# Decode attention over 537 MB of K and V: the first tile in halves with K in two pieces, and three halvings on VectorE in the last three tiles

## The chip, the cores and the metric

One core of one Trainium2 chip. The metric is device time in microseconds (us) of a whole execution; a run states the median of its timed executions. Each changed kernel was timed in alternating rounds with the kernel before on the same chip.

## The reference

```
B, H, Sq, Skv, Dh = 8, 32, 1, 4096, 128          # q, k, v in bf16
scores = einsum('bhqd,bhkd->bhqk', q, k) * Dh**-0.5
attn   = softmax(scores)
out    = einsum('bhqk,bhkd->bhqd', attn, v)
```

One query per head against 4096 keys: every byte of K and V is read once, 536.9 MB in all, and hardly any arithmetic is done per byte.

## The kernel before

A tile is eight heads: K and V are 8.39 MB each (128 partitions x 256 rows x 128), and there are 32 tiles. VectorE multiplies K by q and halves the products by additions; TensorE sums the rest with an identity matrix into PSUM; VectorE reduces that to scores; ScalarE makes the weights; TensorE multiplies V by them. K and V share a pool of three buffers.

```
SLOTS = 3                                          # K and V tiles in flight, in one pool
cuts = {
    ("k", 0): [C // 4, C // 4, C // 2],            # C = 256 rows of a partition
    ("k", NT - 2): [C // 2] * 2,
    ("k", NT - 1): [C // 4, C // 4, C // 2],
    ("v", NT - 1): [C // 2, C // 4, C // 8, C // 16, LAST // 2, LAST // 4, LAST // 4],
}
def load(kind, t):                                 # on the SP queue
    ...
        dma = nc.sync.dma_start(buf[:, c0 : c0 + n, :], src[t, :, c0 : c0 + n, :])
        ...
        if kind == "k" and t == 0 and c0 == n:     # q goes out behind the first piece of K
            nc.sync.dma_start(q_all[:], q_n)

def width_of(t, lo):                               # halve on VectorE down to this width
    return D // 8 if lo == C // 2 and 0 < t < NT - 3 else D // 2

def product(t, lo, hi):                            # VectorE: K*q, then the halvings
    ...
def sum_over_d(t, lo, hi):                         # TensorE: width/ds matmuls, ds = 512/(hi-lo)
    ...

for t in range(NT):
    loop = 0 < t <= LT                             # LT = NT - 3
    if not loop:                                   # tile 0 and the last two
        if t + 1 < NT: load("k", t + 1)
        load("v", t)
    first = HALF if loop else Q
    product(t, 0, first)
    ...
    if loop:                                       # halves
        sum_over_d(t, 0, HALF); product(t, HALF, C); sum_over_d(t, HALF, C)
        scores_of(t, 0, HALF)
        values_loop(t - 1)
        load("k", t + 1)
        load("v", t)                               # needs the buffer of K of tile t
        scores_of(t, HALF, C)
    else:                                          # quarters
        ...
    weights_of(t)
```

## Time and profile before

| | before |
|---|---|
| device time, median (range of 6) | 1250.97 us (1250.81 to 1251.15) |
| span of the profiled execution | 1249.5 us (its device time: 1251.34) |
| HBM traffic | 536.94 MB read, 430 GB/s over the span |
| busy: VectorE, TensorE, ScalarE | 81%, 61%, 13% |
| DMA | nine tenths or more in all slices but the last |

How to read it: 430 GB/s averaged over the whole span is nearly the 433.5 GB/s of the steady stretch. The lines for this are in the prediction.

### The profile page before, as it was taken

The page shows a single profiled execution, that of the slowest core. Times are in us where ns is not written, and L with a number is a line of the kernel's source. Part 1 is how long each engine was busy: PE and PEld are TensorE (multiplying, and loading weights), DVE is VectorE, ACT ScalarE, POOL GpSimd, SP SyncE. Part 2 cuts the span into 40 slices and gives each one's busy share as a digit, 9 for nine tenths or more (in the row PEclk, how much of TensorE's full clock was granted, in tenths as well). Part 3 has the DMA queues.
Part 4 walks back from the last instruction along what each step waited for, and adds up shares of the span by engine and source line. Part 5 has one row for each costly group of instructions (what it writes and reads, how often), then busy time and mean ns, then how long its engine had stood idle before and what let it go on. Part 6 is the DMA issues. An engine that isn't in the chain of part 4 may idle for free. (4 is left out here: it accounts for less than half of the span.)

```text
span 1249.5 us, 10534 instructions
## 1 busy us (share of the span) xinstructions
PE 761.4 (61%) x3004; PEld 284.3 (23%) x3004; DVE 1010.6 (81%) x379; ACT 166.1 (13%) x433; POOL 4.5 (0%) x24
## 2 busy tenths in 40 slices
PE   3356457554586555766557665577655676556855
PEld 1122122221222212222122222122221222212312
DVE  7877987778977789777797777987779877798694
ACT  0111011111011110111101111011110111101111
POOL 1000000000000000000000000000000000000000
PEclk9786798777887777878678777887867877778867
DMA  9999999999999999999999999999999999999998
GB/s 405 436 436 435 436 429 424 426 436 437 436 432 435 435 434 434 435 435 426 431 436 435 426 430 436 435 434 437 433 432 430 433 437 432 433 432 425 429 442 339
DMA packets 11430, 537.30 MB, mean 430 GB/s; under 512 B 1808, under 2 KB 2064, under 8 KB 2320
## 3 DMA queue, kind: packets, MB, share of 16 engines
q1 hardware_dynamic: 11072, 536.94, 99.5%
q8 instruction: 14, 0.23, 0.1%
q10 hardware_dynamic: 336, 0.07, 0.0%
q14 instruction: 8, 0.07, 0.0%
HBM read 536.94 MB, written 0.07 MB: 430 GB/s over the span
## 5 line engine op out<-in xcount | busy, mean ns | idle before, releaser
L189 DVE TENSOR_TENSOR kt<-kt,qb 128x16384 bf16<-128x16384 bf16 (+1 forms) x70 | 556.8, 7955 | 156.8 <-DMA kt<-in_k_dram 150.1
L207 PE MATMUL ps<-kt,ident 128*128 128x512 bf16 x688 | 253.2, 537 | 416.3 <-DVE kt L195 415.9
L290 PE MATMUL av<-vt,w 128*32 x1740 | 425.3, 397 | 4.4
L195 DVE TENSOR_TENSOR kt<-kt 128x4096 bf16<-128x4096 bf16 (+1 forms) x126 | 382.7, 3037 | 4.3
L290 PEld LDWEIGHTS av<-vt,w 128*32 x1740 | 173.3, 100 | 262.1 <-issue 118.9
L207 PEld LDWEIGHTS <-ident 128*128 128x128 bf16 x688 | 80.0, 125 | 583.0 <-DVE kt L195 444.7
L244 ACT ACTIVATE e<-sc,nmax 128x256 bf16<-128x256 f32 x32 | 16.2, 508 | 708.0 <-DVE nmax L238 708.0
L251 ACT ACTIVATE w<-e,mine 128x256 bf16<-128x256 bf16 x256 | 105.6, 495 | 1.1
L219 DVE TENSOR_REDUCE sc<-ps 128x128 f32<-128x512 f32 (+1 forms) x70 | 48.1, 687 | 57.0 <-PE ps L207 57.0
L347 ACT ACTIVATE comb<-av 32x512 bf16<-32x512 f32 (+1 forms) x32 | 18.8, 586 | 327.3 <-PEq L280 320.9
L276 PE MATMUL av<-vt,w 128*32 128x512 bf16 x116 | 47.1, 498 | 14.5 <-issue 13.3
L367 PE MATMUL op<-comb,pick 32*16 32x128 bf16 (+1 forms) x128 | 12.2, 213 | 21.9 <-ACT comb L347 21.9
L276 PEld LDWEIGHTS av<-vt,w 128*32 128x32 bf16 x116 | 6.9, 101 | 54.7 <-issue 54.7
L175 PE MATMUL qp<-qg,heads 8*128 8x128 bf16 x32 | 7.0, 217 | 16.7 <-ACT qg L173 16.7
L367 PEld LDWEIGHTS <-pick 32*16 32x16 bf16 (+1 forms) x128 | 8.7, 83 | 28.9 <-issue 28.5
L231 DVE TENSOR_REDUCE pmax<-sc 128x1 f32<-128x256 f32 x32 | 13.4, 420 | 1.1
L318 PE MATMUL av<-vt,w 128*32 128x512 bf16 x188 | 13.7, 417 | 0.0
L173 ACT ACTIVATE qg<-qh 8x128 bf16<-8x128 f32 x32 | 8.5, 267 | 33.5 <-PE qh L169 33.5
L169 PE MATMUL qh<-q_all,ident 128*8 128x128 bf16 x32 | 7.2, 225 | 8.7 <-DMA q_all<-in_q_dram 8.3
L177 ACT ACTIVATE qb<-qp 128x128 bf16<-128x128 f32 x32 | 8.9, 278 | 9.7 <-PE qp L175 9.7
L339 DVE RECIPROCAL rz<-zp 16x1 f32<-16x1 f32 x16 | 2.3, 147 | 8.1 <-PE zp L332 8.1
L233 DVE TENSOR_SCALAR spread<-same,pmax 128x32 f32<-128x32 f32 x32 | 7.7, 242 | 1.1
(30 smaller groups left out, 45.7 us busy)
## 6 DMA issues: line engine op xcount, KB each, us to landing
kt<-in_k_dram SPq DMA_DIRECT2D x4, 4096.0 KB, 23.8
kt<-in_k_dram SPq DMA_DIRECT2D x4, 2048.0 KB, 12.3
vt<-in_v_dram SPq DMA_DIRECT2D x1, 4096.0 KB, 33.1
vt<-in_v_dram SPq DMA_DIRECT2D x1, 2048.0 KB, 37.6
vt<-in_v_dram SPq DMA_DIRECT2D x1, 1024.0 KB, 39.7
vt<-in_v_dram SPq DMA_DIRECT2D x1, 512.0 KB, 40.5
vt<-in_v_dram SPq DMA_DIRECT2D x31, 26.2
kt<-in_k_dram SPq DMA_DIRECT2D x29, 28.7
```

The source lines that it names most:

```text
L189: nc.vector.tensor_tensor(out=part, in0=part, in1=qb[:].to_broadcast([P, hi - lo, D]), op=ALU.mult)
L195: nc.vector.tensor_tensor(out=part[:, :, 0:n], in0=part[:, :, 0:n], in1=part[:, :, n : 2 * n], op=ALU.add)
L207: nc.tensor.matmul(ps[:], lhsT=ident[:], rhs=kt[:, lo:hi, s * ds : (s + 1) * ds], start=(s == 0), stop=(s == n - 1),)
L219: made = nc.vector.tensor_reduce(out=scs[t][:, lo:hi], in_=ps, axis=AX.X, op=ALU.add)
L231: nc.vector.tensor_reduce(out=pmax[:], in_=sc[:], axis=AX.X, op=ALU.max)
L244: nc.scalar.activation(out=e[:], in_=sc[:], func=ACT.Exp, bias=nmax[:, 0:1], scale=scale, accum_out=esums[t // R][:, t % R : t % R + 1],)
L251: nc.scalar.activation(out=w[:, :, g, :], in_=e_g, func=ACT.Copy, scale=mine[:, 0, g : g + 1])
L276: pe.matmul(av, lhsT=wf[:, i * nw : (i + 1) * nw], rhs=vf[:, i * nv : (i + 1) * nv], **how)
L290: pe.matmul(av, lhsT=wf[:, bass.ds(ow + i * nw, nw)], rhs=vf[:, bass.ds(ov + i * nv, nv)], start=False, stop=False,)
L318: nc.tensor.matmul(avs[t][j * AG : (j + 1) * AG, :], lhsT=w[:, i, :, :], rhs=vt[:, c0 : c0 + CB, :], start=(i < TG), stop=(j not in group[ ...
L347: nc.scalar.activation(out=comb[0:n, :, :], in_=av[0:n, :, :], func=ACT.Copy)
L367: nc.tensor.matmul(ops[n][:], lhsT=pick[0:e, m, r, :], rhs=comb[0:e, m, :], start=(r == 0 and m == 0), stop=(r == R - 1 and m == CB - 1 an ...
```

## The change

Its intent: tile 0 takes the form of the tiles in the loop (two halves, the second with three halvings), so that VectorE and TensorE do fewer small pieces there, and the last three tiles trade slow waits for TensorE (16 or 8 matmuls) for short additions on VectorE.

```
-        ("k", 0): [C // 4, C // 4, C // 2],
+        ("k", 0): [C // 2] * 2,
...
-        return D // 8 if lo == C // 2 and 0 < t < NT - 3 else D // 2
+        return D // 8 if lo == (C // 2 if t <= LT else 3 * C // 4) else D // 2
...
+            halves = t <= LT
             loop = 0 < t <= LT
...
-            first = HALF if loop else Q
+            first = HALF if halves else Q
...
-            if loop:
+            if halves:
                 sum_over_d(t, 0, HALF)
                 product(t, HALF, C)
                 sum_over_d(t, HALF, C)
                 scores_of(t, 0, HALF)
...
-                values_loop(t - 1)
-                load("k", t + 1)
-                load("v", t)
+                if loop:
+                    values_loop(t - 1)
+                    load("k", t + 1)
+                    load("v", t)
                 scores_of(t, HALF, C)
```

q still goes out behind the first piece of K, which is now 4 MB instead of 2 MB.

More of the change, by code (lines that the diff above doesn't have):

```diff
@@ L129 @@
     nc.gpsimd.memset(w_last[:], 0.0)
+    LT = NT - 3
     loads = {}
@@ L299, in values_loop @@
         loops.append(loop)
-    LT = NT - 3
     def values_of(t, lo, hi):
@@ L404 @@
                 load("v", t)
-            first = HALF if loop else Q
+            first = HALF if halves else Q
             product(t, 0, first)
-            if not loop:
+            if not halves:
                 sum_over_d(t, 0, first)
@@ L440 @@
                 values_of(t - 1, 0, C)
-            if not loop:
+            if not halves:
                 scores_of(t, HALF + Q, C)
```

## The prediction

> **What bounds the kernel now.** I read the page's top first: which engine is full.
>
> ```profile
> PE 761.4 (61%) x3004; PEld 284.3 (23%) x3004; DVE 1010.6 (81%) x379; ACT 166.1 (13%) x433; POOL 4.5 (0%) x24
> DMA  9999999999999999999999999999999999999998
> HBM read 536.94 MB, written 0.07 MB: 430 GB/s over the span
> ```
>
> No compute engine is full, and the DMA engines are busy in every slice. VectorE's 81% is near enough that I checked whether it ever holds the transfers up. The idle time ahead of each tile's first product says no: in the steady state VectorE waits for K.
>
> ```profile
> 81.31 8.69 DVE L189 TENSOR_TENSOR kt<-kt,qb 128x16384 bf16<-128x16384 bf16 x1 [5.14 <-DMA kt<-in_k_dram]
> 121.38 8.69 DVE L189 TENSOR_TENSOR kt<-kt,qb 128x16384 bf16<-128x16384 bf16 x1 [6.61 <-DMA kt<-in_k_dram]
> 160.12 8.69 DVE L189 TENSOR_TENSOR kt<-kt,qb 128x16384 bf16<-128x16384 bf16 x1 [5.28 <-DMA kt<-in_k_dram]
> ```
>
> Five microseconds of slack per tile, tiles 38.7 us apart. The semaphore landings in the trace give the rate: one 8.39 MB tile of K or V every 19.35 us, 433.5 GB/s, from the second tile to the last, with no pause. In the packet records each of the 16 DMA engines starts a 64 KiB packet as the previous one ends (2.42 us each). So the kernel is one uninterrupted stream from 1.8 us (first packet) to about 1246 us (last V piece landed), plus what comes after. The chain that ended last says the same:
>
> ```profile
> 1204.83 40.66 DMA vt<-in_v_dram
> 1245.48 0.04 issue
> 1245.53 0.83 PE op L359 x12
> 1246.36 0.22 PE op L367 x4
> 1246.58 0.24 PE op L359 x4
> 1246.82 0.02 issue
> 1246.84 0.36 ACT stage L378
> ```
>
> After the last data come a few small matmuls, one copy and the store: 3.4 us to the end of the span.
>
> So only three things can move the time: a hole in the stream (a load issued after the queue has run dry), the speed of the slowest DMA engine, and the tail after the last landing. The change works at the start and in the last three tiles, so those are the two places to look for holes. The start:
>
> ```profile
> 8.32 0.26 PE L169 MATMUL qh<-q_all,ident 128*8 128x128 bf16 x1 [8.32 <-DMA q_all<-in_q_dram]
> 9.55 4.43 DVE L189 TENSOR_TENSOR kt<-kt,qb 128x8192 bf16<-128x8192 bf16 x1 [6.66 <-ACT qb L177]
> 41.17 0.33 SPq L156 DMA_DIRECT2D kt<-in_k_dram  x1
> 42.77 8.65 DVE L189 TENSOR_TENSOR kt<-kt,qb 128x16384 bf16<-128x16384 bf16 x1
> 74.50 0.33 SPq L156 DMA_DIRECT2D vt<-in_v_dram  x1
> ```
>
> VectorE begins when q has come, at 9.55. Tile 1 at 42.77 waits for no data; tiles 0 and 1 run back to back at VectorE's own pace. The load of V for tile 1 (74.50) needs the buffer of K of tile 1, so it is tied to that pace. What is queued ahead of it, K of tile 2, has its last packets end at 80.61 to 80.93, by engine. Slack now: 6.1 us. In the steady state the same distance is fixed by landings and stays as it is.
>
> **What the Trainium skill says.** "DMA: Bandwidth & Descriptors", section "Where 436 GB/s comes from", puts the fabric's ceiling at 435.2 GB/s; the 433.5 measured here agree, so nothing is to be gained in mid-stream. The same page, "Queues, rings and completion order", says that each DMA engine takes the descriptors of a ring in order. The trace agrees: q, queued behind the first 2 MB of K, lands at 8.28, 0.23 us after that piece (8.05). "Runtime: NRT & Kernel Launch", section "Instruction fetch mechanics", says instructions are fetched in 16 KiB blocks and that crossing a block is mostly hidden. The trace has 14 such packets on the instruction queue, but each pushes back one of the 16 engines by about 1.5 us; by the end the engines stand 3.2 us apart, and several of the late ones carry two fetches. "TensorE: Matmul & The Clock Gate", Part 1, says that the array falls to half clock when idle: the clock is 0.50 around 1241 us here and 1.00 from 1244.6 on.
>
> **Part 1, tile 0.** It has three effects.
> - q is queued behind 4 MB in place of 2 MB. One 2 MB piece takes 4.89 us (landings 8.28 to 13.18), so q lands near 13.15, and VectorE starts 1.27 us later as now (8.28 to 9.55): 14.4 in place of 9.55, that is 4.85 later.
> - Halves in place of quarters. Tile 1 already has this form: 31.73 us from its first product (42.77) to the freeing of its K buffer (74.50). Tile 0 now takes 41.17 - 9.55 = 31.62 to the same point. Equal: the two more halvings (2.29 + 1.22) are paid by fewer fixed costs, fewer small reductions and a 1.9 us wait for 4 matmuls at the end in place of 3.6 us for 8.
> - 12 matmuls fewer on TensorE, which is not on this path.
>
> So everything in tiles 0 and 1 moves by 5.0: K buffer of tile 0 freed at 46.1 (the stream is filled until about 61, harmless), tile 1 begins at 47.7, and V of tile 1 is issued at 47.7 + 31.73 = 79.45. First packets follow an issue by 1.0 us at the start (0.81 to 1.82) and 0.84 in the last store (1247.23 to 1248.07), so by 80.3 to 80.45, against engines running dry at 80.61 to 80.93. The slack goes from 6.1 us to some 0.2 us: just enough, or just not. Cold first packets of 16 KiB took 1.1 us in place of 0.61, so a queue refilled at the last moment may lose up to half a microsecond. I put **+0.3 us** (0 to 0.8). Afterwards: VectorE ends tile 1 at 76.17 + 5 = 81.2 and K of tile 2 comes at 81.3, so the 5 us of idle time swallow the delay whole. K of tile 3 moves from 91.26 to about 96.3, but V of tile 1 fills the stream until 100.0. From tile 2 on it is the old schedule.
>
> **Part 2, the last three tiles.** The form by shape gives halvings of 4096 elements 2.292 us and of 2048 1.225; a straight line through them puts 1024 at 0.69. Waits of a reduction for the matmuls before it:
>
> ```profile
> 1155.74 6.47 PE L207 MATMUL ps<-kt,ident 128*128 128x512 bf16 x16 [9.43 <-DVE kt L195]
> 1162.26 0.69 DVE L219 TENSOR_REDUCE sc<-ps 128x128 f32<-128x512 f32 x1 [5.90 <-PE ps L207]
> 1196.02 3.40 PE L207 MATMUL ps<-kt,ident 128*128 128x512 bf16 x8 [3.67 <-DVE kt L195]
> 1239.23 0.40 PE L318 MATMUL av<-vt,w 128*32 128x512 bf16 x3
> ```
>
> - Tile 29: VectorE +2.29 + 1.22 = +3.5; 16 matmuls (6.5 us) become 4 (1.9), -4.6. Net -1.1.
> - Tiles 30 and 31: +1.22 + 0.69 = +1.9 each; 8 matmuls (3.5) become 2 (1.0, as 0.43 per matmul and 0.18), -2.5. Net -0.65 each.
> - Sum: the last weights are ready about 2.4 us sooner, and the values matmuls of the last tile begin near 1236.8 in place of 1239.23. Loads tied to these tiles are issued 1 to 1.7 us sooner, but none is late now: K of tile 31 goes out at 1179.18 and is needed at 1183.9, V of tile 30 at 1199.45 and needed near 1203.
>
> What is that worth at the end? The last V pieces land at 1243.61, 1244.81, 1245.48, 1245.80 and 1246.12, and the last four values matmuls cannot start before 1244.81; today they start within 0.1 us of it, because TensorE catches up just then. So the 2.4 us become waiting on TensorE: **0 to -0.1 us**. On the other side, a TensorE that waits may be at half clock when the last pieces come; now it is warm from 1244.6. Four values matmuls, four gathering ones and the last four at half clock are worth +0.2 to +0.5, with perhaps one chance in three: **+0.1**.
>
> **Part 3, instruction stream.** 72 fewer entries on TensorE (24 in tile 0, 24 in tile 29, 12 in each of tiles 30 and 31). A block is 256, so fetches shift but hardly change in number, and the engines delayed twice before 1100 stay so: **-0.1**, if the fetch of 1243.3 disappears.
>
> Sum: 1250.9 + 0.3 + 0.1 - 0.1 - 0.05, about **1251.1 us**.
>
> **The rivals.**
> - *The tail was the bound, and the shorter path through the last weights pays.* For it: the chain starts in the matmuls of tile 30, and TensorE works without a break from 1239.2 to 1245.4. Against it: the landings above. It would give 1248.5 to 1250.
> - *A true hole at 80 us.* For it: slack of 0.2 us worked out from numbers good to some 0.3. If q came later still or the first packets took 2 us, the hole would be 1 to 2 us: 1252 to 1253. Every tile behind it keeps the delay, since the stream never catches up.
> - *VectorE becomes the bound in the last tiles* (7.3 us more work). Against: each addition is smaller than the wait that it takes away, on the same chain. It would need the matmul wait to be hidden; worth +2 at most.
>
> **Range and chances.** The runs of before lie within 0.3 us. The start term spans 0 to +0.8, the tail -0.1 to +0.5, fetches ±0.3: 1250.4 to 1252.2 for 8 in 10. A 2% change is 25 us; nothing in either part is of that size.
>
> **What would show it.** First product of tile 0 near 14.4, waiting for q; tile 1 near 47.7; V of tile 1 issued near 79.4; tile 2 beginning within 0.5 us of 81.3, now with almost no idle time before it, and tile 3 with its 6 us again. If the idle time before tile 3 begins over 1 us later than 121.4, there was a hole. Near the end: reductions waiting 1.9 us or less in tile 29, values matmuls of tile 31 from about 1237 and then waiting for DMA; last landing near 1246.3. I am wrong if the last landing moves by over 1 us, or if the span moves without it.

## The result, and the profile after

The changed kernel took **1252.41 us** (median of 6, 1252.04 to 1253.42) against 1250.97 for the kernel before: 1.44 us more. The ratio is 1.0012, 95% interval 1.0 to 1.0025. (A ratio is the mean time of one kernel's runs over that of the other's of the same rounds, so not quite the ratio of the medians quoted.) The predicted range ended at 1252.2.

The head of its page. VectorE has two instructions more and TensorE 36 matmuls fewer; the stream is still the bound.

```profile
PE 745.0 (60%) x2968; PEld 277.8 (22%) x2968; DVE 1019.6 (82%) x381; ACT 166.0 (13%) x433; POOL 4.4 (0%) x24
HBM read 536.94 MB, written 0.07 MB: 429 GB/s over the span
```

The start, from the timeline of the changed kernel (start us, duration us, engine, line, operation; in brackets the idle time before it and what ended it):

```profile
13.25 0.26 PE L170 MATMUL qh<-q_all,ident 128*8 128x128 bf16 x1 [13.25 <-DMA q_all<-in_q_dram]
14.47 8.69 DVE L189 TENSOR_TENSOR kt<-kt,qb 128x16384 bf16<-128x16384 bf16 x1 [11.59 <-ACT qb L178]
...
47.81 8.65 DVE L189 TENSOR_TENSOR kt<-kt,qb 128x16384 bf16<-128x16384 bf16 x1
...
79.55 0.33 SPq L157 DMA_DIRECT2D vt<-in_v_dram  x1
...
81.14 8.65 DVE L189 TENSOR_TENSOR kt<-kt,qb 128x16384 bf16<-128x16384 bf16 x1
...
121.92 8.69 DVE L189 TENSOR_TENSOR kt<-kt,qb 128x16384 bf16<-128x16384 bf16 x1 [7.38 <-DMA kt<-in_k_dram]
```

VectorE starts 4.9 us later, tile 1 begins at 47.81, V of tile 1 is issued at 79.55 and tile 2 begins at 81.14 with no idle time at all, all within 0.15 us of the prediction. But VectorE then waits 7.38 us for K of tile 3. The landings show why: the first of the sixteen DMA engines has landed its share of K of tile 2 at 80.49 and of V of tile 1 at 100.79, which is 20.30 us later; in the kernel before it is 19.35 (80.98 to 100.33). The last engine is no measure of this: it needed 20.47 us here (80.97 to 101.44), but 20.65 in the kernel before too (81.29 to 101.94), where a block of instructions held it up near 98 us.

The end, from the chain that ended last (start, duration, what) and then from TensorE's part of the timeline:

```profile
1205.07 40.82 DMA vt<-in_v_dram
...
1245.94 0.83 PE op L357 x12
1246.77 0.22 PE op L365 x4
1246.99 0.24 PE op L357 x4
...
1247.25 0.36 ACT stage L376
```

```profile
1241.58 1.89 PE L316 MATMUL av<-vt,w 128*32 128x512 bf16 x16 [1.88 <-DMA vt<-in_v_dram]
1244.05 0.62 PE L316 MATMUL av<-vt,w 128*32 128x512 bf16 x8 [0.59 <-DMA vt<-in_v_dram]
1245.28 0.40 PE L316 MATMUL av<-vt,w 128*32 128x512 bf16 x4 [0.61 <-DMA vt<-in_v_dram]
...
1245.94 0.83 PE L357 MATMUL op<-vt,w_last 128*16 128x128 bf16 x12 [0.26 <-DMA vt<-in_v_dram]
```

TensorE now waits for V four times where it had none of those waits before: the time saved ahead of the last weights has become waiting. The last landing of V moved from 1246.12 to 1246.55; in e6 below, an execution without a hole that took 1250.77 us, it came at 1245.67. The final store took 1.76 us from issue (1247.64) to landing (1249.40), 1.34 before (1247.23 to 1248.57).

### The profile page after: what moved, and what is told of

Same layout as the page of the kernel before. It is cut to its first block, busy times and chain, and to the rows that moved or that the text cites. A ratio compares the mean times of both kernels' runs of the same rounds, so it can differ in the third digit from the quotient of the medians.

```text
span 1250.5 us, 10463 instructions
## 1 busy us (share of the span) xinstructions
PE 745.0 (60%) x2968; PEld 277.8 (22%) x2968; DVE 1019.6 (82%) x381; ACT 166.0 (13%) x433; POOL 4.4 (0%) x24
## 5 line engine op out<-in xcount | busy, mean ns | idle before, releaser
L207 PE MATMUL ps<-kt,ident 128*128 128x512 bf16 x652 | 235.0, 527 | 427.6 <-DVE kt L195 427.2
L195 DVE TENSOR_TENSOR kt<-kt 128x8192 bf16<-128x8192 bf16 (+2 forms) x132 | 393.2, 2979 | 4.5
L207 PEld LDWEIGHTS <-ident 128*128 128x128 bf16 x652 | 73.9, 122 | 581.8 <-DVE kt L195 430.3
L316 PEld LDWEIGHTS <-w 128*32 128x32 bf16 x188 | 6.4, 114 | 12.3 <-issue 9.9
```

The source lines that it names most:

```text
L195: nc.vector.tensor_tensor(out=part[:, :, 0:n], in0=part[:, :, 0:n], in1=part[:, :, n : 2 * n], op=ALU.add)
L207: nc.tensor.matmul(ps[:], lhsT=ident[:], rhs=kt[:, lo:hi, s * ds : (s + 1) * ds], start=(s == 0), stop=(s == n - 1),)
L316: nc.tensor.matmul(avs[t][j * AG : (j + 1) * AG, :], lhsT=w[:, i, :, :], rhs=vt[:, c0 : c0 + CB, :], start=(i < TG), stop=(j not in group[ ...
```

## The experiments

Twelve kernels ran; all were correct. Only for e3 and e4 does the 95% interval of the ratio lie clear of 1. The argument below therefore rests on medians with their ranges (the kernel before stayed between 1250.76 and 1251.46 in all rounds) and on the traces. Two theories at first: **H**, a hole in the stream near 80 us, and **T**, the tail.

### The start alone, and the tail alone

e1 is the changed kernel with the old widths in the last three tiles; e2 is the kernel before with only the new widths there.

```
e1:  return D // 8 if lo == C // 2 and t < NT - 3 else D // 2
e2:  return D // 8 if t > 0 and lo == (C // 2 if t <= LT else 3 * C // 4) else D // 2
```

> The first tile in halves with K in two pieces, the last three tiles as before. Theory H (a hole in the stream near 80 us: V of tile 1 is issued at 79.5, 0.95 us before its first packets, against engines that run dry from 80.04; first packets take 3.2 in place of 2.42 us; 1.1 us in all): 1251.9 to 1252.2 us, tile 3 beginning near 121.9 after over 7 us of idle time. Rival T (the tail costs the time: later or cold matmuls, or the last instruction fetch at 1247.4 colliding with the final store): 1250.8 to 1251.3.

Measured: 1252.23 us (1252.04 to 1253.32) against 1250.93, ratio 1.0012. V of tile 1 was issued at 79.80, and tile 3 began at 122.21 after 7.40 us of idle time. As H has it, 0.03 us above its range: the start alone carries 1.30 us of the 1.44.

> Only the last three tiles changed, tile 0 as before. H: no hole, V of tile 1 issued near 74.5, 1250.8 to 1251.3 us, the values matmuls of the last tile waiting for DMA as in the changed kernel. T: 1251.8 or more, the last landing of V near 1246.1 but the end of the span 1 us or more later than before.

Measured: 1251.63 us (1251.32 to 1252.05) against 1250.93. No hole (V of tile 1 at 74.50), yet 0.7 us lost; neither theory expected that. The two parts together would make 2.0 us, and the whole change costs 1.44. The tail's 0.7 us is taken up below.

### Two attempts to close the hole

Both bring q earlier, so that VectorE starts on the landing of the first half of K.

```
e3:  -            if kind == "k" and t == 0 and c0 == n: nc.sync.dma_start(q_all[:], q_n)
     +    nc.sync.dma_start(q_all[:], q_n)         # ahead of load("k", 0)
e5:  -        ("k", 0): [C // 2] * 2,
     +        ("k", 0): [C // 4, C // 4, C // 2],
```

> The changed kernel with q loaded ahead of K. VectorE then starts on the landing of the first half of K, near 13.3 in place of 14.47, and V of tile 1 is issued near 78.4, 1.7 us or more ahead of the dry point. H: the hole closes, 1251.0 to 1251.5 (what is left would be the tail's 0.4). T: 1252.2 to 1252.5, unchanged.

> The changed kernel with K of tile 0 in three pieces as before (quarter, quarter, half), so that q lands at 8.3; the products stay in halves. VectorE starts near 13.3 (second quarter landed at 13.18). H: as with q first, 1251.0 to 1251.5, V of tile 1 issued near 78.4. T: 1252.2 to 1252.5. If it is the halves themselves and not q behind 4 MB that cost the time, it stays at 1252.2 or more although q is early.

Measured: e3 1253.78 us (1253.35 to 1255.38), e5 1253.02 (1251.67 to 1253.39), against 1250.93. Both medians are above the changed kernel's, though V of tile 1 is issued *earlier* (79.03 and 78.43); e5's range overlaps with that of the changed kernel. Theory H as I held it, with a fixed delay of about 1 us from issue to first packet, fell here. e5's timeline:

```profile
78.43 0.33 SPq L157 DMA_DIRECT2D vt<-in_v_dram  x1
```

```profile
81.03 8.69 DVE L189 TENSOR_TENSOR kt<-kt,qb 128x16384 bf16<-128x16384 bf16 x1 [0.92 <-DMA kt<-in_k_dram]
...
121.85 8.69 DVE L189 TENSOR_TENSOR kt<-kt,qb 128x16384 bf16<-128x16384 bf16 x1 [7.38 <-DMA kt<-in_k_dram]
```

The issue comes 1.66 us ahead of the first engine's running dry (80.09), and still the wait for K of tile 3 is as long as in the changed kernel. The packet records say what happened: eleven engines went on without a pause or nearly, but the last began V of tile 1 at 82.44, 4.0 us after the issue. In the changed kernel all sixteen were empty by 80.50 and began between 80.50 and 81.42, 0.95 to 1.9 us after the issue. So I formed theory **L**: what counts is how far ahead of the dry point that load is issued, and the lead it needs is not 1 us but several. The rival, **S**: the loss belongs to tile 0's new shape.

### A delay alone, in four sizes

The kernel before, with idle reductions on VectorE in tile 0 (their result is not used) and nothing else changed. The number of elements and repeats sets the delay.

```
             product(t, 0, first)
+            for x in [32] if t == 0 else []:      # e6; [32]*2 e7; [32]*3 e8; [32]*4+[4] e9
+                nc.vector.tensor_reduce(out=idle[:, 0:x],
+                    in_=same[:]....to_broadcast([P, x, TB]), axis=AX.X, op=ALU.max)
```

> The kernel before, with one idle reduction of about 1.2 us on VectorE in tile 0 (its result is not used); nothing else changed. V of tile 1 is issued near 75.7, more than 4 us before the first DMA engine runs dry (80.1 to 80.6). Theory L (what counts is how late that load is issued, and an issue needs up to 4 us to reach the last engine, as the run with three pieces showed): 1250.8 to 1251.3, unchanged. Rival S (the loss belongs to the new shape of tile 0, its pieces or halves): 1250.8 to 1251.2 in all four delayed kernels.

> The same with two idle reductions. V of tile 1 near 76.9, some 3.2 us or more before the first engine runs dry. L: between nothing and one microsecond, 1250.9 to 1252.0, a few engines starting late. S: 1250.8 to 1251.2.

> The same with three idle reductions. V of tile 1 near 78.1, as in the changed kernel with K in three pieces (78.43). L: 1252.0 to 1253.4, engines starting unevenly, the landing of V of tile 1 spread over more than 1.3 us though no instruction fetch lies between. S: 1250.8 to 1251.2.

> The same with four and a short one, 5 us in all. V of tile 1 near 79.5, as in the changed kernel (79.55). L: 1251.9 to 1252.6, all engines empty at 80.0 to 80.6 and starting again together about 1 us after the issue; less lost than with three reductions, odd as that is. S: 1250.8 to 1251.2.

Measured, against 1250.87 us: e6 1250.82 (1250.76 to 1251.03), e7 1251.12 (1250.93 to 1251.21), e8 1252.42 (1251.19 to 1253.02), e9 1252.43 (1252.37 to 1252.47). All four fall where L puts them. e6 and e7 would fit S as well; e8 and e9 rule it out, since the old shape of tile 0 with 3 or 5 us of delay costs as much as the new one. In e8 the cost differs much from one execution to the next.

The table puts all kernels in order of the issue of V of tile 1. "Dry" is when the first and the last engine finish K of tile 2, "started" when the first and the last begin V of tile 1, both from the packet records of one profiled execution. "Lost" is the end of the latest first packet of V, less what it would be without a pause (last dry + 2.42).

| kernel | V issued | dry | started | lost, us | median less its before, us |
|---|---|---|---|---|---|
| before | 74.50 | 80.61 to 80.93 | 80.61 to 80.94 | 0 | 0 |
| e6 | 75.73 | 80.09 to 80.57 | 80.10 to 80.57 | 0 | -0.05 |
| e7 | 76.92 | 80.21 to 80.49 | 80.22 to 80.49 | 0.3 | +0.25 |
| e8 | 78.04 | 80.08 to 80.51 | 80.09 to 81.45 | 1.5 | +1.55 |
| e5 | 78.43 | 80.09 to 80.48 | 80.10 to 82.44 | 2.1 | +2.09 |
| e3 | 79.03 | 80.42 to 81.17 | 80.42 to 82.43 | 2.0 | +2.85 |
| e9 | 79.53 | 80.09 to 80.42 | 80.48 to 81.14 | 1.3 | +1.56 |
| changed | 79.55 | 80.03 to 80.50 | 80.50 to 81.42 | 1.3 | +1.44 |
| e1 | 79.80 | 79.99 to 80.75 | 80.77 to 81.51 | 1.3 | +1.30 |
| e4 | 89.29 | 80.04 to 80.55 | 90.24 to 90.97 | 10.9 | +11.04 |

A lead of 4.4 us costs nothing, 3.3 us next to nothing, and from 2.0 us down it costs 1.3 to 2.1. It isn't monotonic: worst is an issue 1.4 to 1.7 us before the dry point. There the engines start unevenly, and the slowest sets the end: averaged over the sixteen engines, the loss is only 0.2 in e8, 0.7 in e5 and 0.6 in e3, against 1.1 to 1.4 in e9, the changed kernel and e1. When all are empty they start within 1 us of each other, but their first packets take 2.6 to 3.6 us in place of 2.42 (3.0 to 3.3 in the changed kernel for all but one). In e3 a further 0.6 us come from the last engine's dry point, 81.17: with q first, the first half of K landed at 13.85 and not at 13.23, as in e5.

### The large dose: K of tile 0 in one piece

```
e4:  -        ("k", 0): [C // 2] * 2,
     +        ("k", 0): [C],
```

> The changed kernel with K of tile 0 in one piece: q lands near 23.1, VectorE starts near 24.4 and V of tile 1 is issued near 89.4, long after the engines ran dry (80.1 to 80.5). L (the hole is the issue, plus about 1 us to the first packet, plus 0.75 us of a cold first packet, less the dry time): a hole of 10.3 to 11 us that is never made good, 1261 to 1262.5 us. If the slack of 5 us per tile could give part of it back, 1256 or so.

Measured: 1261.97 us (1261.74 to 1262.5) against 1250.93, so +11.04 for a hole of 10.9. In its timeline:

```profile
89.29 0.33 SPq L157 DMA_DIRECT2D vt<-in_v_dram  x1
```

```profile
131.81 8.69 DVE L189 TENSOR_TENSOR kt<-kt,qb 128x16384 bf16<-128x16384 bf16 x1 [7.50 <-DMA kt<-in_k_dram]
```

Tile 3 begins 10.4 us later than before (121.38), and the 27 tiles in which VectorE waits 5 us or more for K give nothing back. VectorE's slack repairs VectorE's delays, never the stream's.

### What the tail alone cost

Theory F: e2 adds six instructions to VectorE (the changed kernel only two, as tile 0 loses four), and an 8 KiB block of instructions that came after the end (1250.9) before now comes at 1215.9. e10 adds six tiny reductions to the kernel before while VectorE waits for q, where they take no time. e11 is e2 with 24 repeated small matmuls, to restore TensorE's own count.

```
e10: +            for _ in range(6 if t == 0 else 0): nc.vector.tensor_reduce(out=idle[:], ...)
                  product(t, 0, first)
e11:              for _ in range(1 + (2 if 6 <= t < 18 else 0)):
                      nc.tensor.matmul(qh[:], lhsT=ident[:, p0 : p0 + G], rhs=q_all[:, x, :], ...)
```

> The kernel before with six tiny reductions on VectorE while it waits for q, so with the six instructions more that the changed last tiles bring, and no time lost. Theory F (the tail alone cost 0.7 us because the 8 KiB block of instructions that came at 1250.9, after the end, now comes near 1216 and holds up one DMA engine): such a packet near 1216 to 1219, 1251.2 to 1251.8 us. Rival W (the tail's cost is in its longer VectorE work or in a TensorE that waits): 1250.8 to 1251.1.

> The changed last three tiles alone, with 24 small matmuls repeated in tiles 6 to 17, so that TensorE's instruction count is that of before. If the later fetches of TensorE's own blocks (1234.1 and 1245.8 in place of 1219.6 and 1243.3) made the 0.7 us: 1250.9 to 1251.2. If VectorE's extra block did (F): still 1251.3 to 1251.8. W: 1251.6.

Measured, against 1250.93: e10 1251.75 us (1251.34 to 1251.92), e11 1251.64 (1251.34 to 1251.94). e10 reproduces e2's loss with no change in the tail at all; restoring TensorE's count changes nothing. The queue lines of the DMA view (queue: packets, MB, share), first of the kernel before, then of e10:

```profile
q14 instruction: 8, 0.07, 0.0%
```

```profile
q14 instruction: 9, 0.07, 0.0%
```

One packet more, 8 KiB, at 1215.8 in e10. On the engine it fell to it made a pause of 0.31 us and the next packet 0.66 us longer, and that engine had already been held up by two 16 KiB blocks (near 214 and 992 us); it then finished last, at 1226.43 where the next ones finished at 1225.5 (its last full-size packet). In e2 and e11 too the engine that took this block finished last (1226.55 and 1226.65, the next ones 1225.8 and 1225.95). So the tail's longer VectorE work and earlier weights are worth nothing that these runs can tell, and e2's 0.7 us come from six instructions' place in the count. It is e10 that shows this: e11's median would fit rival W as well. In the changed kernel the block comes at 1250.8, after the end.

This touches the delay runs too, for their idle reductions are also added instructions. e9, like e10, has a ninth block:

```profile
q14 instruction: 9, 0.07, 0.0%
```

It came at 1218.9, on the engine that then finished last (1227.18, the next one 1226.71), so up to 0.5 us of e9's 1.56 may be the block's. e8's ninth block came at 1246.3, on an engine that was not the last. The holes near 80 us, 1.5 and 1.3 us in the packet records, lie ahead of both blocks, and e1, e5 and the changed kernel have no such block within their span; so L stands.

### The last fetch and the final store

e12 is the changed kernel with 36 repeated small matmuls (3 in each of tiles 6 to 17, written as in e11).

> The changed kernel with 36 small matmuls repeated in tiles 6 to 17, TensorE's instruction count that of before, so that its last fetch (1247.4, just ahead of the final store) comes near 1244. If that fetch slows the store: 1251.8 to 1252.1. If only the hole counts: 1252.2 to 1252.6.

Measured: 1252.05 us (1251.88 to 1253.63) against 1250.93. The last fetch moved to 1242.5 and the store took 1.34 us (1247.84 to 1249.18). The median is 0.36 us under the changed kernel's, but the two ranges overlap almost wholly, and e3 and e4, whose last fetch also came just ahead of the store, had stores of 1.33 and 1.34 us. There, however, the fetch had ended 0.7 and 0.6 us before the store's first packet, in the changed kernel only 0.1 us before. e12's median lies in the range forecast for a fetch that slows the store; whether that fetch costs anything stays open.

## Why the prediction was wrong

- **The bound** was right: e4's hole of 10.9 us in the stream came out as 11.04 us of time.
- **When V of tile 1 is issued**: predicted 79.45, measured 79.55. Right, and so was each step to it.
- **What that costs: the step that failed.** "I put +0.3 us (0 to 0.8)." Measured 1.3 in the trace, and 1.30 in e1 by itself. It was mis-sized in two terms. The dry point was taken from one profiled execution of the kernel before, 80.61 to 80.93; in that execution 75 packets between 22 and 62 us took over 2.45 us, worth 0.54 us per engine, and in nine of the thirteen other runs the engines ran dry between 80.0 and 80.6 (80.03 to 80.50 in the changed kernel). Where the prediction had 0.2 us of slack, the engines paused for 0.4 us on average. And the cold first packet cost 0.6 to 0.9 us on nearly all engines, not "up to half a microsecond" on a queue refilled at the last moment. The delay from the issue to the first packet (0.95) was right for the first engine; the last one began 1.9 us after the issue. What happened is my second rival, "a true hole at 80 us", which I had priced at 1252 to 1253 and then given too little weight.
- **The lead.** Working with a slack of 0.2 us supposed that an issue just ahead of the dry point is as good as one far ahead. e8, e5 and e3 show the opposite: it is as bad as an issue on an empty queue, or worse.
- **The hole is never made good**: stated in the rival, right (e4).
- **Its signs of a hole** used the same single trace. Tile 3 began at 121.92, 0.5 us after the 121.4 and not "over 1 us later", and the last landing moved by 0.43 us, not by over 1; neither sign fired, though there was a hole. The kernel before was itself late in that trace, by the slowed packets and by the block near 98 us. Against e6, which has no hole, tile 3 came 0.9 us later (121.06 there) and the last landing 0.88 us later.
- **The last three tiles** bring 0: right. The last tile's values matmuls began 1.7 us sooner (1237.57 against 1239.23; predicted 2.4, where the terms for tiles 30 and 31 add up to -0.6 each and not -0.65), and all of it was spent waiting for V. The fear of a half-clocked TensorE at the end (+0.1) did not come true: the twelve matmuls took 0.83 us in both kernels. (In the kernel before, the granted clock was 1.00 from 1243.5 on, not from 1244.6, as the prediction reads it.)
- **Instruction fetches** (-0.1): the fetch of 1243.3 did not disappear but moved to 1247.4. I took the fetches for noise of ±0.3; e10 shows that one block of 8 KiB can cost 0.8.
- Sum by the runs: hole +1.3 (e1), tail 0, and 0.1 left over. That is a sum of medians; the traces do not close so neatly. Against e6's profiled execution, the changed kernel's has its last landing 0.88 us later and loses 0.5 us more after it, 0.4 of that in the store; in e1 all 1.28 us are there at the last landing (1246.95). The hole delays each engine by a different amount, and which engine ends last also depends on where the blocks of instructions fall. So 1.3 us is what the hole costs in e1, and its share in any one execution of the changed kernel is known less well.

The kernel before remains the fastest version measured; e6 equals it.

## What to carry to other kernels

In a kernel bound by its stream, the distance from issuing a load to the moment the queue runs dry is what to protect; compute slack elsewhere can't buy back a hole. Don't plan that distance down to the issue delay: here 4.4 us were safe and 2 us were not, and an issue in the last two microseconds did as much harm as one on an empty queue, or more. Take such small margins from several executions, for one trace carried a hiccup larger than the margin worked out from it.

## What the Trainium skill lacked or had wrong

- "Runtime: NRT & Kernel Launch", section "Instruction fetch mechanics", calls the cost of crossing a block mostly hidden. For a kernel bound by its loads it is not hidden: a 16 KiB block typically made its DMA engine pause for 1.0 us and its next packet 0.5 us longer, the engines stood 3.2 us apart at the end of the kernel before, and one 8 KiB block more cost 0.8 us of the total (e10).
- "DMA: Bandwidth & Descriptors", section "Latency and other measured facts", gives some 0.6 us to the first byte of a transfer issued from the SP queue. That agrees for the first engine where the engines are empty, if counted from the end of the issue instruction (79.88; first packet at 80.50, the last engine's at 81.42). The page lacks the case of engines about to run dry: up to 4.0 us from issue to the last engine's first packet (e5, 78.43 to 82.44).
- No page found gives the cost of restarting an empty stream: the first 64 KiB packet took 3.0 to 3.3 us on most engines of the changed kernel in place of 2.42. Why a late issue on busy engines spreads more than one on empty engines, no run here settles.
